# Gated linear attention feeding a mixture of experts: reshapes of the first groups on TensorE instead of through DRAM, and seven weight splits moved into the first expert block

## The chip, the cores and the metric

One core of one Trainium2 chip runs the whole program. The metric is the device time of one execution in microseconds (us); lower is better. Engines: PE (TensorE), DVE (VectorE), ACT (ScalarE), POOL (GpSimd), SP (SyncE, which here only issues DMAs).

## The reference

Two stages. The first is a complex-gated linear attention, step by step over time; the second mixes four two-layer experts.

```python
# q, k, v, a_re, a_im: (4, 8, 768, 48) = batch, heads, time, width
mag = np.sqrt(a_re * a_re + a_im * a_im)
scale = np.minimum(mag, 0.999) / (mag + 1e-06)
a_re_n, a_im_n = (a_re * scale, a_im * scale)
for t in range(S):
    new_re = ar * S_re - ai * S_im
    new_im = ar * S_im + ai * S_re
    S_re, S_im = (new_re + k_t v_t^T, new_im)
    y[:, :, t] = q_t^T S_re
x = y.transpose(0, 2, 1, 3).reshape(3072, 384)
p = domain_probs / domain_probs.sum(-1)
for e in range(4):                     # w1: (4, 384, 1024), w2: (4, 1024, 384)
    out += p[:, e:e+1] * (np.maximum(x @ w1[e], 0) @ w2[e])
```

## The kernel before, in words

The 3072 tokens are cut into NG = 12 groups of 256, each of two chunks of 128 steps. For a group the gates are normalised (`norm`, ACT and DVE), multiplied up along time (`prefix`, DVE), and turned into decayed Q and K (`finish`, DVE and ACT). These come out with (head, width) on the partitions in three slabs of 128. The attention wants each head's 48 rows at partitions 0 to 47 (real part) and 64 to 111 (imaginary part), in `Qst` and `Kst`. `finish` gets them there by writing Q and K to DRAM and reading them back (lines 378 and 383): `k_d<-K`, then `Kst<-k_d`.

`attention` then does for each chunk: `increment` (transposes of K, line 411, a copy to `KT`, line 412, and the state's increment, line 416), `scores` (line 430, masked by DVE, line 433) and `values` (lines 442 and 446, copied to `y`, line 454). y goes to DRAM and comes back as x with 128 rows of (head, width) on the partitions (`y_d<-y`, `xa<-y_d`, lines 486 and 135). `split_x` splits x into a rounded high part `xh` (ACT, line 141) and a rest `xl` (DVE, line 142), since the expert matmuls run in a reduced-precision format (fp32r) three times: high by high, low by high, high by low.

The experts run in two phases. In the first, `moe1` takes a group through the 16 slices of the first two experts, as eight steps of `w1_step` (line 152) and `w2_step` (line 171), one block per group. In the second phase, 512 tokens at a time go through the other two (lines 585 and 598). Weights must be split as x is. `split_w` does this for the first 16: ACT rounds (line 115, `whi`), PE computes the difference with an identity and a negated identity into PSUM (lines 125 and 128, `lp`), and ACT copies it out (line 129, `wlo`). All 16 are split before the first block. The staging tiles for a weight are taken from the tags of `PRE`, two buffers each.

Each engine runs its instructions in order; the order comes from a scheduler that works on the program order and the dependencies. `between(k)` puts a piece of the next group's attention ahead of step k of the current block: for group g the pieces start at step max(2, 5 - g).

Of the kernel before, what the change touches and what calls it, by code (L numbers as in the profile page):

```python
# [11 lines left out]
ALU = mybir.AluOpType  # L12
# [17 lines left out]
NST = 4  # L30
# [25 lines left out]
NPRE = 10  # L56
NMID = 12
# [3 lines left out]
def fast_path(ctx, tc, qkP, aP, vP, probsP, w, out, flag):  # L61
# [8 lines left out]
    ident = const.tile([P, P], F32, name="ident")  # L70
    make_identity(nc, ident)
# [16 lines left out]
    nc.gpsimd.dma_start(pr, probsP.rearrange("(n p) e -> p n e", p=P))  # L88
# [5 lines left out]
    wts = {}  # L94

# [16 lines left out]
    def split_w(i, src, ps=None, prev=None, prev_pe=None):  # L112
        hi = wpool.tile([P, 2 * HD], F32R, tag="whi", name=f"whi{i}")
        lo = wpool.tile([P, 2 * HD], F32R, tag="wlo", name=f"wlo{i}")
        ins = nc.scalar.activation(hi, src, AF.Copy)
        if prev is not None:
            behind(ins, prev)
        if ps is None:
            nc.vector.tensor_tensor(lo, src, hi, op=ALU.subtract)
        else:  # L120
            pool, tag = ps
            for u in range(2):
# [10 lines left out]
    def load_x(g):  # L133
        x = moe.tile([P, NJ, G], F32, tag="x", name=f"xa{g}", bufs=1)
        nc.sync.dma_start(x, y_d[g].rearrange("(j p) t -> p j t", p=P))
        return x

    def split_x(g, x):
        xh = moe.tile([P, NJ, G], F32R, tag="xh", name=f"xha{g}")
        xl = moe.tile([P, NJ, G], F32R, tag="xl", name=f"xla{g}")  # L140
        tc.keep_in_program_order(nc.scalar.activation(xh, x, AF.Copy))  # L141
        tc.keep_in_program_order(nc.vector.tensor_tensor(xl, x, xh, op=ALU.subtract))
# [59 lines left out]
    with ExitStack() as c1:  # L202
# [4 lines left out]
        mask = big.tile([P, C], F32, name="mask")  # L207
# [17 lines left out]
        nc.gpsimd.memset(Qst[32:IM], 0.0)  # L225
        nc.gpsimd.memset(Kst[32:IM], 0.0)
        nc.gpsimd.memset(KT, 0.0)
        nc.gpsimd.memset(P2, 0.0)
        nc.gpsimd.memset(TA, 0.0)

# [22 lines left out]
        def tmp(name):  # L253
            return big.tile([P, 2, NJ * G], F32, tag="tmp", name=name, bufs=TMP)

        def cmul(x, br, bi, shape, nm):
# [6 lines left out]
            v1 = tmp(f"{nm}a")[:, :, :n].rearrange(pat, **kw)  # L263
            v2 = tmp(f"{nm}b")[:, :, :n].rearrange(pat, **kw)
# [11 lines left out]
        def norm(g, A, parts=((0, SEG),), prev=(None, None)):  # L276
            s = tmp(f"s{g}")
            u = tmp(f"u{g}")
            for n, (lo, hi) in enumerate(parts):
# [5 lines left out]
                nc.scalar.activation(L, Af[:, 1], AF.Square)  # L285
# [5 lines left out]
                if n > 0:  # L291
                    behind(ins[0], idn)
                nc.scalar.activation(L, m2, AF.Ln, bias=m2b)
                nc.scalar.activation(y0, L, AF.Exp, scale=-0.5)
# [9 lines left out]
        def prefix(g, A, cuts=(1, NS)):  # L304
            for i in range(1, SEG):
# [6 lines left out]
                nc.vector.tensor_tensor(x[:, 1], z[:, 1, 0], z[:, 0, 1], op=ALU.add)  # L312
            k = 1
            while k < NS:
                nb = MS // (2 * k)
                Al = A[:, :, SEG - 1, :].rearrange("p c (b s) -> p c b s", s=2 * k)
                br, bi = (Al[:, c, :, k - 1:k].broadcast_to([P, nb, k]) for c in range(2))
                cmul(Al[:, :, :, k:], br, bi, [nb, k], f"sk{g}_{k}")
                k *= 2
            As = A.rearrange("p c i (j s) -> p c i j s", j=NJ)  # L320
# [5 lines left out]
        def finish(g, A, qk, parts=((0, CG),)):  # L326
            Q = big.tile([P, 2, NR, C + 1], F32, tag="tmp", name=f"Q{g}", bufs=TMP)
            K = big.tile([P, 2, NR, C], F32, tag="K", name=f"K{g}", bufs=1)
            s = tmp(f"s2{g}")
            u = tmp(f"u2{g}")  # L330
# [19 lines left out]
            for lo, hi in parts:  # L350
# [11 lines left out]
                if hi == CG:  # L362
                    nc.scalar.activation(Q[:, :, :, C].rearrange("p c (j n) -> p c j n", n=CG)[:, :, :, lo:],
                                         A[:, :, SEG - 1, NS - 1::NS].unsqueeze(3).broadcast_to([P, 2, NJ, hi - lo]),
                                         AF.Copy)
                a2, i0, t, kn = (some(x, lo, hi) for x in (a2a, i0a, ta, qk[:, 1]))
# [6 lines left out]
                scr = []  # L373
                for x, nm, w in ((Q, "q", C + 1 if hi == CG else C), (K, "k", C)):
                    dt = dram.tile([2, HD, hi - lo, w], F32, name=f"{nm}_d{g}_{lo}")
                    for c in range(2):
                        xs = x[:, c].rearrange("p (j n) t -> p j n t", n=CG)[:, :, lo:hi, :w]
                        nc.sync.dma_start(dt[c].rearrange("(j p) n t -> p j n t", p=P), xs)
                    scr.append(dt)
                for x, dt in zip((Qst, Kst), scr):  # L380
                    eng = nc.gpsimd if g == 0 and x is Qst else nc.sync
                    for c in range(2):
                        landed = eng.dma_start(x[c * IM:c * IM + D, :, lo:hi, :dt.shape[-1]],
                                                   dt[c].rearrange("(h d) n t -> d h n t", d=D))
            return K, last_act, last_dve, landed
# [10 lines left out]
        def chunk(g, c, K, y):  # L396
# [8 lines left out]
            def increment():  # L405
                if last:
                    return
                for i in range(2):
                    kt_ps = ps_a.tile([P, HD], F32, tag="pa", name=f"ktp{g}_{c}_{i}")
                    for j in range(NJ):  # L410
                        nc.tensor.transpose(kt_ps[:, j * P:(j + 1) * P], K[:, i, j * CG + c, :], ident)  # L411
                    nc.scalar.activation(KT[:, :, i * IM:i * IM + D],
                                         kt_ps.rearrange("p (h d) -> p h d", d=D), AF.Copy)
                d_ps = ps_a.tile([M, H, D], F32, tag="pa", name=f"dp{g}_{c}")
# [409 lines left out]
```

## Time and profile before

| what | value |
|---|---|
| median of 3 runs | 1032.83 us (1031.87 to 1033.28) |
| profiled execution, its own time | 1035.97 us |
| span of its instructions | 1034.2 us |
| PE busy | 988.0 us (96%) |
| DVE busy | 596.5 us (58%) |
| ACT busy | 358.9 us (35%) |
| mean granted PE clock | 0.988 of full speed |

The span is the time from the first to the last instruction on the core. The chain that ended last lies on PE for 88% of it and on DMAs for 6%. "Busy" PE counts a matmul from its issue to its modelled end, at whatever clock it was granted. The rows of a timeline give the start, the time up to the end of the last one merged into the row, the engine, the line, and the idle time before it with what ended it.

### The profile page before, as it was taken

What the parts mean: (1) busy time and instruction counts of PE and PEld (TensorE: products, weight loads), DVE (VectorE), ACT (ScalarE), POOL (GpSimd) and SP (SyncE); (2) the same over time, 40 slices, a digit from 0 to 9 for tenths busy, and PEclk for the clock granted to TensorE, in tenths of its full rate; (3) what the DMA queues carried; (4) which work ended last, traced back from release to release, by engine and by line L of the source; (5) the groups of instructions that cost most, each with busy time, mean ns of one, the idle gap of its engine ahead of it and who ended that gap; (6) DMA issues with size and microseconds to landing.
All of it is one profiled execution on the core that took longest, in us unless ns stands there. A gap on an engine that the chain in (4) does not pass through costs nothing.

```text
span 1034.2 us, 15984 instructions
## 1 busy us (share of the span) xinstructions
PE 988.0 (96%) x6522; PEld 920.8 (89%) x6522; DVE 596.5 (58%) x1201; ACT 358.9 (35%) x647; POOL 27.8 (3%) x51
## 2 busy tenths in 40 slices
PE   4599889999999999999999999999999999999997
PEld 2379889898999999999999999999999999999996
DVE  6788877798988998888982264232232232321221
ACT  6845335352634635355342254121111111111110
POOL 4100000000000000000000000000000000000000
PEclk9989999999999999999999999999999999999999
DMA  7837372745658455483653493012030010100000
GB/s 257 217 113 155 107 197 80 191 115 141 165 139 199 120 149 152 120 203 126 145 123 78 129 360 123 1 41 82 1 110 13 22 71 1 61 1 1 31 1 34
DMA packets 79378, 113.12 MB, mean 109 GB/s; under 512 B 5440, under 2 KB 64496, under 8 KB 79296
## 3 DMA queue, kind: packets, MB, share of 16 engines
q1 hardware_dynamic: 76768, 101.61, 35.5%
q0 software_dynamic: 2528, 10.41, 2.8%
q8 instruction: 53, 0.87, 0.4%
q14 instruction: 29, 0.24, 0.1%
HBM read 74.11 MB, written 37.88 MB: 108 GB/s over the span
## 4 chain that ended last, share of the span: by engine, by line
PE 88%; DMA 6%; DVE 3%; ACT 1%; issue 1%; SPq 0%; DVEq 0%; POOL 0%; ACTq 0%; POOLq 0%
PE pob L598 19%; PE phb L585 19%; PE ph L152 18%; PE po L171 17%; PE sc L430 5%; PE dp L416 2%; PE yp L446 2%; PE yp L442 2%; DMA Kst<-k_d 2%; DMA k_d<-K 1%; PE ktp L411 1%; PE lp L125 1%; DMA pr<-probsP 1%; DMA q_d<-Q 1%; DMA xa<-y_d 1%
## 5 line engine op out<-in xcount | busy, mean ns | idle before, releaser
L591 DVE SCALAR_TENSOR_TENSOR hlb<-phb,hhb 128x512 fp32r<-128x512 f32 x96 | 66.3, 691 | 247.2 <-ACT hhb L590 247.2
L590 ACT ACTIVATE hhb<-phb 128x512 fp32r<-128x512 f32 x96 | 57.4, 598 | 314.2 <-PE phb L585 299.9
L171 PE MATMUL po<-whi,hh 128*128 128x384 f32 x384 | 129.2, 339 | 1.1 <-ACT hh L161 1.1
L598 PE MATMUL pob<-wlo,hhb 128*128 128x384 f32 x384 | 129.3, 337 | 0.0
L171 PE MATMUL po<-wlo,hh 128*128 128x384 f32 x384 | 129.1, 336 | 0.0
L598 PE MATMUL pob<-whi,hhb 128*128 128x384 f32 x384 | 128.9, 336 | 0.0
L171 PE MATMUL po<-whi,hl 128*128 128x384 f32 x384 | 123.1, 338 | 0.5 <-DVE hl L162 0.5
L598 PE MATMUL pob<-whi,hlb 128*128 128x384 f32 x384 | 117.8, 336 | 0.0
L152 PE MATMUL ph<-xha,whi 128*128 128x256 f32 x576 | 105.6, 288 | 4.1 <-ACT xha L141 4.1
L161 ACT ACTIVATE hh<-ph 128x512 fp32r<-128x512 f32 x96 | 57.2, 596 | 149.7 <-PE ph L152 146.1
L152 PE MATMUL ph<-xla,whi 128*128 128x256 f32 x576 | 103.5, 286 | 0.0
L152 PE MATMUL ph<-xha,wlo 128*128 128x256 f32 x576 | 101.4, 284 | 0.0
L162 DVE SCALAR_TENSOR_TENSOR hl<-ph,hh 128x512 fp32r<-128x512 f32 x96 | 66.0, 688 | 51.0 <-ACT hh L161 50.3
L152 PEld LDWEIGHTS ph<-xha,whi 128*128 128x128 f32 x576 | 87.2, 191 | 6.2 <-ACT xha L141 4.9
L585 PE MATMUL phb<-xhb,whi 128*128 128x512 f32 x288 | 91.8, 392 | 0.0
L152 PEld LDWEIGHTS ph<-xla,whi 128*128 128x128 f32 x576 | 83.6, 192 | 0.7 <-issue 0.6
L152 PEld LDWEIGHTS ph<-xha,wlo 128*128 128x128 f32 x576 | 83.2, 191 | 0.2 <-issue 0.2
L585 PE MATMUL phb<-xlb,whi 128*128 128x512 f32 x288 | 83.4, 392 | 0.0
L585 PE MATMUL phb<-xhb,wlo 128*128 128x512 f32 x288 | 82.1, 393 | 0.0
L598 PEld LDWEIGHTS pob<-wlo,hhb 128*128 128x128 f32 x384 | 72.1, 188 | 3.5
L598 PEld LDWEIGHTS pob<-whi,hhb 128*128 128x128 f32 x384 | 72.1, 188 | 3.4
L171 PEld LDWEIGHTS po<-whi,hh 128*128 128x128 f32 x384 | 72.6, 189 | 1.6 <-ACT hh L161 1.4
(142 smaller groups left out, 1568.9 us busy)
## 6 DMA issues: line engine op xcount, KB each, us to landing
wst<-w SPq DMA_DIRECT2D x32, 384.0 KB, 4.8
qk<-qkP SPq DMA_DIRECT2D x24, 384.0 KB, 7.0
acc_d<-acc POOLq DMA_DIRECT2D x24, 384.0 KB, 4.5
prev<-acc_d SPq DMA_DIRECT2D x24, 384.0 KB, 4.8
q_d<-Q SPq DMA_DIRECT2D x22, 387.0 KB, 3.8
Qst<-q_d SPq DMA_DIRECT2D x22, 387.0 KB, 5.6
A<-aP SPq DMA_DIRECT2D x22, 384.0 KB, 8.7
k_d<-K SPq DMA_DIRECT2D x22, 384.0 KB, 3.0
```

Source lines behind the costliest of these rows:

```text
L152: ins = nc.tensor.matmul(ph[:, u, :], wt[:, j * P:(j + 1) * P], xt[:, j, :], start=(n == 0), stop=(n == 3 * NJ - 1))
L161: nc.scalar.activation(hh, ph, AF.Relu)
L162: nc.vector.scalar_tensor_tensor(hl, ph, 0.0, hh, op0=ALU.max, op1=ALU.subtract)
L171: nc.tensor.matmul(po[t], ht[:, u, t * P:(t + 1) * P], wt[:, HD:], start=(i % FE == 0 and n == 0), stop=(i % FE == FE - 1 and n == 2))
L416: ins = nc.tensor.matmul(d_ps[:, h, :], KT[:, h, :], vc[:, h * D:(h + 1) * D], start=True, stop=True)
L430: nc.tensor.matmul(s_ps[:, h, :], Kc[:, hf * 4 + h, :], Qc[:, hf * 4 + h, :], start=True, stop=True)
L442: ins = nc.tensor.matmul(yo, state[g, c][:, h, :], Qc[:, h, :], start=True, stop=False)
L446: ins = nc.tensor.matmul(yo, vc[:, h * D:(h + 1) * D], sc[h // 4][:, h % 4, :], start=first, stop=True)
L585: nc.tensor.matmul(ph, wt[:, j * P:(j + 1) * P], xt[:, j, :], start=(n == 0), stop=(n == 3 * NJ - 1))
L590: nc.scalar.activation(hh, ph, AF.Relu)
L591: nc.vector.scalar_tensor_tensor(hl, ph, 0.0, hh, op0=ALU.max, op1=ALU.subtract)
L598: nc.tensor.matmul(po[t], ht[:, t * P:(t + 1) * P], wt[:, HD:], start=(i % FE == 0 and n == 0), stop=(i % FE == FE - 1 and n == 2))
```

## The change

- **Q and K of the first two groups.** New `pick` multiplies by a 48-column slice of a wide identity (`wide`), 20 matmuls for eight heads, and moves a chunk's rows to their place in PSUM; ACT copies them to `Qst` or `Kst`. Partitions 32 to 63 of PSUM are first set by `blank`, a matmul with a row of zeros, 512 columns wide. For K of a group's first chunk, `turned_back` transposes `KT` back instead. This holds for group 0 (Q of chunk 0, K of both) and group 1 (K of both); Q of chunk 1 of group 0 and all Q of group 1 keep their trip through DRAM (`trip`). `near_attention` orders the pieces. The other groups are as before.
- **x of the first three groups.** New `turn_x` makes x from y by six matmuls with slices of a band matrix per chunk, into PSUM, and `split_x` reads that. `values` has a `blank` per chunk for these groups and copies y once and not in two halves.
- **Weights.** Nine are split ahead of the first block, seven in it, two in front of each of its steps, staged in the two buffers of the tag `acc` alone. The splits ahead of it use two PSUM pools instead of one.
- **Order.** The probabilities' DVE work moves behind the first group's K. `prefix` and `finish` of the first two groups work chunk by chunk. Attention pieces of groups 1 to 4 start at steps 5, 4, 3 and 2. The transposes and the increment of chunk 1 of each group move behind x, for group 0 behind the start of the first block.

```diff
-NPRE = 10
-NMID = 12
+NPRE = 9
+NSEL = 2
+XSEL = 3
+FIRST = {1: 5, 2: 4, 3: 3, 4: 2}
+HOFF = 96
...
+        def blank(ps):
+            n, w = ps.shape[1:]
+            nc.tensor.matmul(ps[32:IM], zero, ident[0:1, 0:1].unsqueeze(2).broadcast_to([1, n, w]),
+                             start=True, stop=True)
+
+        def pick(g, nm, X, dst, s, w):
+            n = 4 if w == C else 3
+            for h0 in range(0, H, n):
+                hs = range(h0, min(h0 + n, H))
+                ps = ps_a.tile([M, len(hs), w], F32, tag="pa", name=f"{nm}p{g}_{s}_{h0}")
+                blank(ps)
+                for h in hs:
+                    js = [j for j in range(NJ) if -D < h * D - j * P < P]
+                    for j in js:
+                        o = 32 + h * D - j * P
+                        for c in range(2):
+                            nc.tensor.matmul(ps[c * IM:c * IM + D, h - h0, :], wide[:, o:o + D],
+                                             X[:, c, j * CG + s, :w], start=(j == js[0]), stop=(j == js[-1]))
+                nc.scalar.activation(dst[:, h0:h0 + len(hs), s, :w], ps, AF.Copy)
...
+            def turned_back():
+                for h0 in range(0, H, 4):
+                    ps = ps_a.tile([M, 4, C], F32, tag="pa", name=f"kp{g}_{c}_{h0}")
+                    for h in range(4):
+                        nc.tensor.transpose(ps[:, h, :], KT[:, h0 + h, :], ident)
+                    nc.scalar.activation(Kst[:, h0:h0 + 4, c, :], ps, AF.Copy)
...
+        def turn_x(g, c, y):
+            xp = ps_a.tile([P, NJ, C], F32, tag="pa", name=f"xp{g}_{c}")
+            for j in range(NJ):
+                ps = [p for p in range(HP) if -HOFF < 2 * D * p - P * j < P]
+                for p in ps:
+                    o = HOFF - (2 * D * p - P * j)
+                    state["xp"] = nc.tensor.matmul(xp[:, j, :], band[:, o:o + P], y[:, p, c * C:(c + 1) * C],
+                                                   start=(p == ps[0]), stop=(p == ps[-1]))
+            return slice(c * C, (c + 1) * C), xp
+
+        def near_attention(g, QK):
...
+            if g == 0:
+                pick(g, "q", Q, Qst, 0, C)
+                yield
+                landed = trip(f"q_d{g}", Q, Qst, 1)()
+            else:
+                landed = trip(f"q_d{g}", Q, Qst)()
+            yield landed
+            turn0()
+            back0()
+            sc0()
+            yield
+            pick(g, "k", K, Kst, 1, C)
+            inc0()
+            val0()
+            sc1()
+            xs = [turn_x(g, 0, y)]
+            val1()
+            xs.append(turn_x(g, 1, y))
+            yield xs
...
                 def between(k, g=g, pieces=pieces, first=first, last=last):
+                    if g == 1:
+                        for i in range(NPRE + 2 * k, min(NPRE + 2 * k + 2, NF1)):
+                            split_w(i, stage1(i, ("acc",)), ((ps_a, "pa"),) * 2, *late)
```

What this does to the order on the engines, at three places. On PE, around the first group's attention, before (`ktp`: transposes of K, `dp`: increment, `lp`: a weight's split, `sc`: scores):

```order
L411 MATMUL ktp_0_0_480<-ident,K_291 128x128 x3
L411 MATMUL ktp_0_1_485<-ident,K_291 128x128 x3
L416 MATMUL dp_0_490<-v_0_476,KT 112x48 x8
L125 MATMUL lp_0_601<-wst_596,ident 128x384
L125 MATMUL lp_1_605<-wst_596,ident 128x384
L430 MATMUL sc_0_0_501<-Qst,Kst 128x128 x4
L430 MATMUL sc_0_1_508<-Qst,Kst 128x128 x4
```

and now (`qp` and `kp_1`: `pick`; line 474: `turned_back`; line 355: `blank`):

```order
L369 MATMUL qp_0_0_304<-Q_235,wide 48x128 x9
L369 MATMUL qp_0_4_317<-Q_235,wide 48x128 x9
L466 MATMUL ktp_0_0_360<-wide,K_236 128x128 x3
L466 MATMUL ktp_0_1_365<-wide,K_236 128x128 x3
L474 MATMUL kp_0_0_370<-wide,KT 112x128 x4
L474 MATMUL kp_0_4_376<-wide,KT 112x128 x4
L494 MATMUL sc_0_0_382<-Qst,Kst 128x128 x4
L494 MATMUL sc_0_1_389<-Qst,Kst 128x128 x4
L355 MATMUL kp_1_0_401<-wide,zero 32x512
L355 MATMUL kp_1_4_414<-wide,zero 32x512
```

The scores now follow transposes of `KT` and not a reading of K from DRAM, and the pieces of `pick` and `blank` stand behind them, ahead of the increment. On ACT, what stands ahead of the copies that these scores wait for (lines 475), now:

```order
L467 ACTIVATE KT<-ktp_0_0_360 128x8x48
L467 ACTIVATE KT<-ktp_0_1_365 128x8x48
L405 ACTIVATE u_234<-s_233,a2b 128x24x16
L406 ACTIVATE u_234<-u_234,a2e 128x24x16
L308 ACTIVATE s_496<-A_204 128x768
L475 ACTIVATE Kst<-kp_0_0_370 112x4x128
L475 ACTIVATE Kst<-kp_0_4_376 112x4x128
```

Two steps of the second chunk's reciprocal (lines 405 and 406) and one square of the next group's gates (line 308) stand between the copies to `KT` and those to `Kst`. On PE behind the first steps of the first block (`ph`: first layer, `po`: second layer), now:

```order
L165 MATMUL ph_1_855<-xla_612,whi_543 128x256 x3
L482 MATMUL dp_1_633<-v_1_302,KT 112x48 x8
L135 MATMUL lp_0_783<-wst_778,wide 128x384
L138 MATMUL lp_0_783<-whi_780,nident 128x384
L135 MATMUL lp_1_787<-wst_778,wide 128x384
L138 MATMUL lp_1_787<-whi_780,nident 128x384
L135 MATMUL lp_0_796<-wst_791,wide 128x384
L138 MATMUL lp_0_796<-whi_793,nident 128x384
L184 MATMUL po_0_0_827<-whi_510,hh_0_823 128x384
```

The second increment of group 0 and the first late split, which stood ahead of the block, now stand between its first and its second layer.

## Rows read from the trace of the kernel before

**Rows 1.** The page, busy time by engine, its row on PE.

```profile
PE 988.0 (96%) x6522; PEld 920.8 (89%) x6522; DVE 596.5 (58%) x1201; ACT 358.9 (35%) x647; POOL 27.8 (3%) x51
```

**Rows 2.** Windows: stretch, length, PE, PEld, DVE, ACT, POOL busy, granted clock, DMA.

```profile
51.50:57.80 6.30, 6.30 (x29) 6.30 (x30) 4.09 (x5) 0.87 (x2) 0.00 (x0) 0.50 0.88 277
...
153.40:156.80 3.40, 3.40 (x18) 2.82 (x17) 2.82 (x8) 0.00 (x0) 0.00 (x0) 0.50 0.52 209
...
245.60:623.90 378.30, 377.55 (x3041) 369.11 (x3041) 290.04 (x600) 165.98 (x305) 9.23 (x17) 1.00 0.56 154
```

**Rows 3.** Timeline from the first group's K to the first block: start, us, engine, line.

```profile
24.17 0.85 ACT L129 ACTIVATE wlo<-lp 128x384 fp32r<-128x384 f32 x2
...
36.14 0.62 ACT L357 ACTIVATE u<-s,a2b 128x384 f32<-128x384 f32 x1
...
36.77 1.03 DVE L371 TENSOR_TENSOR K<-A,u 128x384 f32<-128x384 f32 x2
...
37.31 0.83 ACT L284 ACTIVATE s<-A 128x768 f32<-128x768 f32 x1
...
38.79 0.87 ACT L412 ACTIVATE KT<-ktp 128x384 f32<-128x384 f32 x2
...
39.76 1.74 PE L416 MATMUL dp<-v,KT 128*112 128x48 f32 x16 [1.27 <-issue]
...
51.47 3.76 PE L430 MATMUL sc<-Qst,Kst 112*128 112x128 f32 x16 [8.61 <-DMA Kst<-k_d]
...
74.27 0.62 PE L152 MATMUL ph<-xha,whi 128*128 128x256 f32 x3 [1.45 <-ACT xha L141]
```

**Rows 4.** Timeline: halves of weight splits, and single 384-column passes in fp32r.

```profile
70.17 0.81 PE L125 MATMUL lp<-wst,ident 128*128 128x384 f32 x2
...
70.99 0.83 PE L125 MATMUL lp<-wst,ident 128*128 128x384 f32 x2
...
120.42 0.33 PE L171 MATMUL po<-whi,hh 128*128 128x384 f32 x1
120.59 0.33 PE L171 MATMUL po<-wlo,hh 128*128 128x384 f32 x1
```

**Rows 5.** Timeline: scores at the full clock, and what PE starts behind them.

```profile
103.40 2.02 PE L430 MATMUL sc<-Qst,Kst 112*128 112x128 f32 x16
105.35 0.43 PE L442 MATMUL yp<-Qst,G 112*48 112x128 f32 x4
```

**Rows 6.** Timeline: matmuls 48 columns wide, and a transpose between them.

```profile
62.13 0.39 PE L446 MATMUL yp<-scs,v 128*48 128x128 f32 x4
...
62.35 0.39 PE L442 MATMUL yp<-Qst,G 112*48 112x128 f32 x4
...
62.67 0.33 PE L411 MATMUL ktp<-ident,K 128*128 128x128 f32 x1
...
62.93 0.43 PE L446 MATMUL yp<-scs,v 128*48 128x128 f32 x4
```

**Rows 7.** Timeline: PE's waits behind the start of the first block.

```profile
124.25 0.61 PE L152 MATMUL ph<-xha,whi 128*128 128x256 f32 x3 [2.63 <-ACT xha L141]
...
129.96 0.44 PE L171 MATMUL po<-whi,hh 128*128 128x384 f32 x1 [1.15 <-ACT hh L161]
...
131.43 0.62 PE L171 MATMUL po<-whi,hl 128*128 128x384 f32 x2 [0.51 <-DVE hl L162]
...
151.88 2.36 PE L430 MATMUL sc<-Qst,Kst 112*128 112x128 f32 x16 [2.85 <-DMA Kst<-k_d]
...
196.27 2.43 PE L430 MATMUL sc<-Qst,Kst 112*128 112x128 f32 x16 [2.08 <-DMA Kst<-k_d]
...
242.15 3.65 PE L430 MATMUL sc<-Qst,Kst 112*128 112x128 f32 x16 [1.52 <-issue]
```

**Rows 8.** Timeline of DVE: K of the third group.

```profile
139.94 1.82 DVE L371 TENSOR_TENSOR K<-A,u 128x768 f32<-128x768 f32 x2
```

**Rows 9.** The page, DMA issues: count, size, median us to landing.

```profile
wst<-w SPq DMA_DIRECT2D x32, 384.0 KB, 4.8
```

More of the change, by code (lines that the diff above doesn't have):

```diff
@@ L29 @@
 E1 = 2
-NST = 4
+NST = 6
 TMP = 4
@@ L120, in split_w @@
         else:
-            pool, tag = ps
-            for u in range(2):
+            for u, (pool, tag) in enumerate(ps):
                 us = slice(u * HD, (u + 1) * HD)
@@ L372, in finish, with trip, back @@
                                                        op=ALU.mult)
[L373 to L385, printed above, removed]
+                return last_dve
+            return Q, K, head, tail
+        def trip(nm, X, dst, lo=0, hi=CG):
+            w = X.shape[-1] if hi == CG else C
+            dt = dram.tile([2, HD, hi - lo, w], F32, name=nm)
+            for c in range(2):
+                nc.sync.dma_start(dt[c].rearrange("(j p) n t -> p j n t", p=P),
+                                  X[:, c].rearrange("p (j n) t -> p j n t", n=CG)[:, :, lo:hi, :w])
+            def back():
+                for c in range(2):
+                    landed = nc.sync.dma_start(dst[c * IM:c * IM + D, :, lo:hi, :w],
+                                               dt[c].rearrange("(h d) n t -> d h n t", d=D))
+                return landed
+            return back
         def t_factors():
@@ L403, in chunk, with turned @@
             sc = []
-            def increment():
-                if last:
+            def turned():
+                if last and g >= NSEL:
                     return
@@ L451, in values @@
                     state["pe"] = ins
-                for u in range(2):
-                    us = slice(u * IM, u * IM + D)
+                for us in ((slice(0, M),) if g < XSEL else (slice(0, D), slice(IM, M))):
                     nc.scalar.activation(y[us, :, cs], y_ps[us], AF.Copy)
-            return increment, scores, values
+            return turned, turned_back, increment, scores, values
         def rotate(g):
@@ L486, in attention @@
                 nc.sync.dma_start(yv[u], y[u * IM:u * IM + D])
-            x = load_x(g)
+        def attention(g, QK):
+            y = small.tile([M, HP, G], F32, tag="y", name=f"y{g}")
+            (turn0, _, inc0, sc0, val0), (turn1, _, inc1, sc1, val1) = (chunk(g, c, QK[1], y) for c in range(CG))
+            turn0()
+            inc0()
+            yield sc0()
+            val0()
+            t_factors()
+            xs = [turn_x(g, 0, y)] if g < XSEL else None
+            yield sc1()
+            val1()
+            if g < XSEL:
+                xs.append(turn_x(g, 1, y))
+            store_y(g, y)
+            x = xs or load_x(g)
+            turn1()
             inc1()
@@ L517, in fast_path, with front @@
         qk = load_qk(0)
+        wst.update({i: stage1(i, PRE) for i in range(NST, NST + 2)})
         A.append(load_a(1))
         nrm = norm(0, A[0], parts=halves)
[L520 to L527 removed]
+        cuts = (1, NS // CG, NS)
+        def front(g, A, qk):
+            pre = prefix(g, A, cuts if g < NSEL else (1, NS))
+            Q, K, head, tail = finish(g, A, qk)
+            if g >= NSEL:
+                next(pre, None)
+                la = head(0, CG)
+                ld = tail(0, CG)
+                backs = [trip(f"{nm}_d{g}", X, st) for nm, X, st in (("q", Q, Qst), ("k", K, Kst))]
+                return (Q, K), la, ld, [back() for back in backs][-1], None
+            pieces = near_attention(g, (Q, K))
+            for c in range(CG):
+                next(pre)
+                la = head(c, c + 1)
+                if g == 0 or c == CG - 1:
+                    landed = next(pieces)
+            for c in range(CG):
+                ld = tail(c, c + 1)
+                r = next(pieces) if g == 0 else None
+            return r, la, ld, landed, pieces
+        x, todo = {}, {}
+        x[0], la, ld, landed, todo[0] = front(0, A[0], qk)
+        norm(1, A[1], prev=(la, ld))
+        for i in range(NPRE):
+            split_w(i, wst[i] if i in wst else stage1(i, PRE), ((ps_o, "po"), (ps_h, "ph")))
+        x[0] = split_x(0, x[0])
+        for _ in todo.pop(0):
+            pass
+        late = wts["x"], state["xp"]
+        behind(nc.vector.reduce_sum(prs, pr, axis=mybir.AxisListType.X), ld)
         nc.vector.tensor_scalar(prs, prs, 1e-9, None, op0=ALU.add)
```

152 lines of the change are left out of this document (88 added, 64 removed).

## The prediction

> **What bounds the kernel now.** I read the page first: PE is busy for 988.0 of 1034.2 us [rows 1], so no change to another engine helps unless it removes one of PE's waits, and PE work that is added costs its full time wherever PE never waits. Then the windows: from 245.6 us on PE waits for 0.75 us in 378 [rows 2], and the second phase is denser still. So all that can be won lies ahead of about 246 us. There I read the timeline of PE for two things. One is when the first block starts, which is the first `ph`: 74.27 us [rows 3]. The reader should see the two long trips ahead of it. K is ready at 36.77 + 1.03 = 37.80, and the scores start at 51.47, after 8.61 us in which PE waits for `Kst`; and x comes back from DRAM just ahead of 74.27. The other is what PE waits for behind that start [rows 7]: 2.63, 1.15 and 0.51 us at the second block's start, then 2.85, 2.08 and 1.52 us for the K of groups 2, 3 and 4. Behind each of the last three the granted clock falls to 0.50 for 3.4 us; one such window stands in [rows 2], and there are three. At half the clock 3.4 us of PE work hold 1.7, so 5.1 us are lost beside the waits. From the first block's start the account is simple: every us of PE work moved behind it is paid, every us of wait removed is won.
>
> **Prices on PE.** Half of a weight's split takes 70.99 - 70.17 = 0.82 us [rows 4], a weight 1.64. A half holds two passes of 384 columns in f32 and one in fp32r. The latter is 0.17, the second layer's spacing [rows 4], so an f32 pass is 0.325. A score pass of 128 columns is (105.35 - 103.40) / 16 = 0.122 [rows 5], an f32 matmul has two of them. Four passes of the 48-column matmuls take 62.35 - 62.13 = 0.22 [rows 6], since two heads run side by side. From these: `pick`, 20 matmuls or 40 passes of the same shape, 2.2 us. `blank`, two f32 passes of 512 columns, no row of its own: 512/384 of 0.325 twice, 0.87; the bounds are 0.24 (two passes at a score's price, were its 32 columns to count) and 1.7 (at half the clock). I take 0.87, since columns streamed set the price of the other f32 rows. `turn_x`, 12 passes with full-width weights at 0.122: 1.46 a chunk. `turned_back`, 8 transposes of one pass, at most 0.122 each: 0.98.
>
> **The first block's start.** The DVE chain up to K has the same steps, so I leave K at 37.80, by 2 us either way: ACT does a split in about 1.7 us (0.85 for the two copies of the low part [rows 3], as much for rounding the same 768 columns), and nine of them stand ahead of that chain's end, about as many as before. In the trace of before the copies to `KT` end at 38.79 + 0.87 = 39.66 [rows 3]. Ahead of `Kst` ACT now has two steps like L357 at 0.62 and one square at 0.83 [rows 3], so it is free at 41.73; the transposes of `KT` hide in that. The first `Kst` copy, 512 wide against 0.44 for 384 in the `KT` row, takes 0.58: scores from 42.3, 9.2 us earlier than 51.47.
>
> From there to `ph`: scores of two chunks 2 x 1.95 = 3.9, four `blank` 3.5, `pick` of K 2.2, the increment 1.6 (16 passes in 1.74 less the end of the last [rows 3]), values 0.9 and 1.8, two `turn_x` 2.9, and two copies that PE waits for with their handoffs (y 0.58, xh 0.43) 1.5. Sum 18.3. Then the clock: after the idle stretch of before, 6.3 us ran at 0.50 [rows 2], a loss of 3.15. Now PE has small pieces, `pick` of Q and the transposes, some 4 us, between the last early split and the scores. The loss lies between 0 and 3.15, and I take 1.6, for no row shows such a mixture. The block starts at 42.3 + 18.3 + 1.6 = 62.2: **12.1 us earlier**. Q by `pick` stands ahead of K and is off this path. The DRAM trip of Q's second chunk starts about 1 us behind K; with the 13.7 us that K's took (37.80 to 51.47), among more loads, it would end near 52.5, and the second chunk's scores come 11 us behind the first, near 53: it hides, without much to spare.
>
> **What is paid behind that start.** Seven weights at 1.64: 11.5. The second increment of group 0, once ahead of the block: 1.6. Group 1: `turned_back` 1.0, `pick` 2.2, four `blank` 3.5, `turn_x` 2.9. Group 2: two `blank` 1.7, `turn_x` 2.9. Together 27.3. Changes between column widths come on top: behind a 48-column pair PE starts a transpose 0.10 us late (62.35 + 0.22 to 62.67), and the next pair 0.14 us late (62.67 + 0.12 to 62.93) [rows 6]. The change adds some five such places, 0.6. Sum **27.9**. The Trainium skill (TensorEngine Tiling (Array Packing), Key Properties) says that a change of tiling mode drains TensorE; the trace agrees, with these 0.10 to 0.14 us. If every one of the some 25 borders of a piece drained, that would be 3 and not 0.6.
>
> ACT's copies for the seven weights, 1.7 us each or 12 in all, hide: ACT is busy for 358.9 of 1034.2 us [rows 1]. Were that cover gone, each would hold up a step of the block. The loads hide too, unless the second rival holds.
>
> **What is won behind it.** Block 1 starts later relative to DVE: DVE's chain for group 1 starts a little earlier than before, and block 0 has 23 us more work. In the trace of before K of group 2 was ready at 141.76 [rows 8], 17.5 us behind the second block's start, and its scores had to wait for the trip. Now DVE has the second chunk's `xl`, two steps and K's own 1.82 left at that start, some 5 us. PE has four first layers and three second layers (12 passes of 0.17, 2.1 us; the first about as long) and two increments ahead of those scores, some 18 us. The trip took 10 us (141.76 to 151.88), so it fits. So the waits of 2.85, 2.08 and 1.52 go, the 0.75 behind 245.6, and the three half-clock windows, 5.1: 12.3. The wait at the second block's start doesn't go wholly. There x of group 1 no longer takes a trip, but `turn_x` of its second chunk stands behind the last second-layer matmul, and ACT has two output copies and two steps of group 3 ahead of that copy to `xh`. Between 0 and the 4.3 of before I take 2.4, so 1.9 are won. Sum **14.2**.
>
> **The sum.** -12.1 + 27.9 - 14.2 = **+1.6 us**. The profiled execution's own 1035.97 would become 1037.6; the median, 3.1 lower, 1034.4. That is no change as far as a measurement of this kernel tells one: 0.2%, 2.1 us.
>
> **Rivals.**
>
> *Faster.* The clock never falls in the first attention, since no idle stretch there is as long as the 8.61 us [rows 3] ahead of the half clock; K comes out 2 us earlier because fewer splits stand in ACT's way; and the wait at the second block's start closes. -1.6 - 2 - 2.4 = -6.0 from the forecast, 1028.4. For it: small pieces break the idle stretch. Against it: they fill less than half of it. Chance 0.30.
>
> *Slower: the loads of the late weights.* Weights 9 to 15 are staged in two buffers alone, so 11 to 15 each wait for the split two before them and then for a load. A load took 4.8 us in the middle of 32 [rows 9], and between a split and the next but one PE has about two splits and one step's layer, 5.4 us. If each of five comes 1.5 us late, PE stops 7.5 us in block 0: 1041.9. It decides from a load of about 5.4 us on. Against it: the queues are quiet then. Chance 0.12.
>
> *Slower: the clock stays down.* The first attention runs at half the clock up to its values, about 10 us instead of 3, and a 1.7 us window follows the second block's start: +5, 1039.5. For it: the first window at 0.50 in [rows 2] lasted 6.3 us of steady work. The Trainium skill (TensorE: Matmul & The Clock Gate, Part 4: PE-mode transpose) says that transposes don't count as PE being busy; by that the 14 transposes of this path would not bring the clock up. No row here shows it alone. Chance 0.15.
>
> *The change doesn't do what it says.* DVE still sets when K of groups 2 to 4 is ready, and the 12.3 us are not won: 1046. Chance 0.04.
>
> **Chances.** The forecast has the remaining 0.39, and I count it as within 0.2%. Faster by over that: 0.30. Slower: 0.12 + 0.15 + 0.04 = 0.31. The range, 1027.5 to 1040, takes in the first rival, most of the clock's, and a spread of 2 us in K; the late loads' upper half and the last rival stay outside.
>
> **What would show it.** Right: first scores near 42, first `ph` at 60 to 64 us, no PE wait for `Kst` at groups 2 to 4, no half-clock window there, a second block that starts 130 to 133 us in against 124.25, and a wait ahead of it between 1 and 3 us. Wrong: scores later than 44 (ACT's queue), `lp` in the first block waiting for `wst`, `blank` away from 0.87, or a granted clock of 0.50 between 45 and 60 us for more than 7.

## The result, and the profile after

The changed kernel takes 1037.03 us (median of 19 runs, 1033.42 to 1039.38), the kernel before 1032.74 us beside it (19 runs, 1029.11 to 1035.51). The ratio is 1.0042, 95% interval 1.003 to 1.0054: slower by 0.4%. The forecast was 1034.4, a loss too small to measure; the time lies in the range, on its slow side.

The profiled execution took 1036.68 us, its span 1035.0. The page's row of busy times, against [rows 1]:

```profile
PE 1012.1 (98%) x6754; PEld 936.9 (91%) x6754; DVE 599.1 (58%) x1217; ACT 361.3 (35%) x656; POOL 24.0 (2%) x50
```

PE is busy for 24 us more, and the span grew by 0.8. Where the two meet is in the timeline of PE (start, us, engine, line, with the idle time before in brackets), from the transposes of K to the first block, then at the second block's start and at the scores of group 4:

```profile
35.78 1.22 PE L466 MATMUL ktp<-wide,K 128*128 128x128 f32 x6 [2.72 <-DVE K L422]
37.58 1.96 PE L474 MATMUL kp<-wide,KT 128*112 128x128 f32 x8 [0.58 <-ACT KT L467]
40.17 3.78 PE L494 MATMUL sc<-Qst,Kst 112*128 112x128 f32 x16 [0.63 <-ACT Kst L475]
43.88 3.62 PE L355 MATMUL kp<-wide,zero 1*32 1x512 f32 x4
47.43 3.69 PE L369 MATMUL kp<-K,wide 128*48 128x128 f32 x40
51.05 1.77 PE L482 MATMUL dp<-v,KT 128*112 128x48 f32 x16
52.75 1.04 PE L355 MATMUL yp<-wide,zero 1*32 1x512 f32 x2
...
61.69 1.60 PE L543 MATMUL xp<-y,band 112*128 112x128 f32 x12 [0.69 <-ACT y L519]
...
63.88 0.62 PE L165 MATMUL ph<-xha,whi 128*128 128x256 f32 x3
...
134.17 0.61 PE L165 MATMUL ph<-xha,whi 128*128 128x256 f32 x3 [0.38 <-ACT xha L152]
...
240.71 2.02 PE L494 MATMUL sc<-Qst,Kst 112*128 112x128 f32 x16 [1.21 <-issue]
```

Against [rows 3]: the scores start at 40.17 instead of 51.47, the first block at 63.88 instead of 74.27. Against [rows 7]: the second block starts at 134.17 instead of 124.25, with 0.38 us of wait instead of 2.63; of the waits for K of groups 2, 3 and 4 only the last is left, 1.21. The windows (length, busy PE, PEld, DVE, ACT, POOL, granted clock, DMA share, GB/s) tell of the clock, against [rows 2]:

```profile
40.20:50.10 9.90, 9.90 (x46) 6.61 (x48) 9.43 (x16) 3.12 (x4) 0.00 (x0) 0.50 0.65 199
50.10:63.80 13.70, 13.01 (x132) 10.44 (x128) 6.95 (x19) 4.75 (x10) 0.00 (x0) 1.00 0.14 35
107.50:114.90 7.40, 7.40 (x69) 4.40 (x69) 4.96 (x20) 1.19 (x2) 0.00 (x0) 1.00 0.01 2
115.00:118.40 3.40, 3.40 (x32) 3.04 (x29) 1.54 (x9) 0.33 (x1) 0.00 (x0) 0.51 0.00 0
135.00:250.00 115.00, 113.73 (x920) 108.65 (x919) 98.07 (x210) 47.08 (x87) 2.17 (x4) 1.00 0.58 153
```

From its first scores on, the first attention runs at half the clock for 9.9 us, with PE busy all the while; a half-clock stretch of 3.4 us at 115 us is new; the three behind the waits for K are gone. Cut at the two block starts, the profiled executions compare as follows (the forecast's terms sorted into the same cuts: of the 27.9 paid, 4.6 belong to group 2 and so to the last row; the 1.9 won at the second block's start stand in the middle one):

| stretch | before | after | change | forecast |
|---|---|---|---|---|
| up to the first block | 74.27 | 63.88 | -10.4 | -12.1 |
| first to second block | 49.98 | 70.29 | +20.3 | +21.4 |
| second block to the end | 909.9 | 900.8 | -9.1 | -7.7 |
| span | 1034.2 | 1035.0 | +0.8 | +1.6 |

So against this profile of the kernel before, the three terms hold to 2 us each. The question for the runs was why the medians differ by 4.3 us where the profiles differ by 0.8, and what each part costs. The ratios below are always to the kernel before, run on the same chip; the changed kernel's own 1.0042 is the number to hold them against. The ratio of the run with selection for one group leaves out one of its six executions, which took 4346 us at a granted clock of 0.221.

### The profile page after: what moved, and what is told of

The parts are those of the page before. It is cut to its first block, busy times and chain, and to the rows that moved or that the text cites. A ratio compares the mean times of both kernels' runs of the same rounds, so it can differ in the third digit from the quotient of the medians.

```text
span 1035.0 us, 16428 instructions
## 1 busy us (share of the span) xinstructions
PE 1012.1 (98%) x6754; PEld 936.9 (91%) x6754; DVE 599.1 (58%) x1217; ACT 361.3 (35%) x656; POOL 24.0 (2%) x50
## 4 chain that ended last, share of the span: by engine, by line
PE 94%; ACT 2%; DVE 2%; DMA 1%; issue 0%; SPq 0%; ACTq 0%
PE pob L737 19%; PE phb L724 19%; PE ph L165 19%; PE po L184 19%; PE sc L494 5%; PE dp L482 3%; PE yp L512 2%; PE yp L508 2%; PE lp L135 2%; PE ktp L466 1%; PE xp L543 1%; DMA wst<-w 1%; PE kp L369 1%; PE yp L355 1%; PE kp L355 1%; DMA q_d<-Q 1%
## 5 line engine op out<-in xcount | busy, mean ns | idle before, releaser
L165 PE MATMUL ph<-xla,whi 128*128 128x256 f32 x576 | 100.8, 283 | 0.0
L184 PEld LDWEIGHTS po<-wlo,hh 128*128 128x128 f32 x384 | 72.5, 189 | 0.5 <-issue 0.2
```

Of the source, the lines that this page charges most:

```text
L165: ins = nc.tensor.matmul(ph[:, u, :], wt[:, j * P:(j + 1) * P], xt[:, j, :], start=(n == 0), stop=(n == 3 * NJ - 1))
L184: nc.tensor.matmul(po[t], ht[:, u, t * P:(t + 1) * P], wt[:, HD:], start=(i % FE == 0 and n == 0), stop=(i % FE == FE - 1 and n == 2))
```

## Experiments

**The kernel before, again.** No edit.

> The kernel before, unchanged, beside itself. The question: its median moved 4.3 us below the changed kernel's, its one profiled execution only 0.8 us (span 1034.2 against 1035.0). Theory: the profiled execution of before was a slow draw, about 3 us over its median, because the executions differ in how long TensorE stays at half its clock; then the spans listed run by run should spread from about 1028 to 1034 us and the granted clock should rise as the span falls. Rival: profiling itself adds these 3 us to this kernel; then the spans of all the timed runs should lie near 1031 with little spread, and a second profile should again show 1034.

Measured: median 1032.57, ratio 0.9992 (0.9976 to 1.0007). The 12 spans reach from 1026.6 us (mean clock 0.990) to 1034.0 (0.985); over all 92 timed runs of this kernel here, span and clock have a correlation of -0.65. The second profile has a span of 1031.3: scores at 50.38, first block at 72.62, second at 122.32. The theory holds in its main part: the first profile was a slow draw, not an effect of profiling. Its reason, the clock, does not explain these two profiles: the slower has the higher clock (0.988 against 0.985), and its first scores, behind the trip of K, come 1.1 us later. By the same three cuts the change is -8.7, +20.6 and -8.2 against this second profile, together +3.7, which is close to the 4.3 of the medians.

**Halves instead of blanks.** Ten of the twelve blanks go, those of K and y; the two of Q stay. (The text before the run says eight of ten; its sum, four and six, counts the ten.) The rows between the halves are zeroed by POOL.

```diff
...
-                blank(ps)
+                if len(parts) == 1:
+                    blank(ps)
...
-                nc.scalar.activation(dst[:, h0:h0 + len(hs), s, :w], ps, AF.Copy)
+                for us in parts:
+                    nc.scalar.activation(dst[us, h0:h0 + len(hs), s, :w], ps[us], AF.Copy)
...
-                if g < XSEL:
-                    blank(y_ps)
...
+        nc.gpsimd.memset(Kst[32:IM], 0.0)
...
+                nc.gpsimd.memset(y[32:IM], 0.0)
```

> The changed kernel without eight of its ten blanks: K of chunk 1 and y are copied out of PSUM in two halves, and the rows between them are zeroed once in SBUF by POOL. Theory: a blank costs PE 0.97 us at the full clock and 1.8 at half, and nothing hides it. Ahead of the first block four of them go, two at half the clock (3.6 + 1.9 us), less about 1 us for a second y copy that PE waits for twice: first block near 59.5 us instead of 63.88. Behind it six go, 5.8 us. Sum about -10 us, 1027. Rival: ACT's four more copies are on the path ahead of the block and the group's border, PE waits instead; then the first block starts at 62 or later and the sum is -6 or less, 1031.

Measured: median 1027.66, ratio 0.9943 (0.9925 to 0.9962): 9.4 us under the changed kernel, as the theory has it, and 0.6% under the kernel before. But not by its own steps: K ended at 40.05, 3.9 later, and the first block started at 61.99, no more than 1.9 earlier. PE's timeline of this run shows one reason, ahead of K:

```profile
9.03 2.90 PE L135 MATMUL lp<-wst,wide 128*128 128x384 f32 x4 [9.03 <-DMA wst<-w]
11.86 3.62 PE L356 MATMUL qp<-wide,zero 1*32 1x512 f32 x4
15.41 2.93 PE L135 MATMUL lp<-wst,wide 128*128 128x384 f32 x4
```

POOL's added zeroing made the row of zeros late, so the two blanks of Q now stand among the early splits (3.62 us at the low clock) and not ahead of them. The greater gain lies behind the block's start: 64.9 us from first to second block instead of 70.29. A blank there costs 0.97 at the full clock, four of them 3.9; and no half-clock stretch came at 115 us (1.7).

**Early blanks back in front.**

```diff
         nc.gpsimd.memset(Qst[32:IM, :, 1:], 0.0)
-        nc.gpsimd.memset(Kst[32:IM], 0.0)
...
                                     compare_op=ALU.not_equal, fill=1.0, base=base, channel_multiplier=1)
+        nc.gpsimd.memset(Kst[32:IM], 0.0)
```

> As the run with copies in halves, but POOL zeroes the rows of Kst behind the band, so that the two blanks of Q, which wait for POOL's row of zeros, stand ahead of the first split again, as in the changed kernel. There the granted clock rose at 12.55 us and K of the first group ended at 36.19; without them in front it rose at 21.27 and K ended at 40.05. Theory: the early blanks bring the clock up some 8 us sooner, the splits and with them ACT's copies run ahead, and K is 3.9 us earlier: first block near 58 us, 1027.7 - 3.9 = 1023.8. Rival: the clock's rise is by chance or K's delay has another cause: K at 40, 1027.7.

Measured: median 1025.56, ratio 0.9923 (0.9897 to 0.9949). K ended at 36.16 and the first block started at 59.01, 3.0 us earlier than in the run before it, but only about 2 of them are left in the median, with ratios whose intervals overlap, and 1.1 in the span: K of group 4 came too late for the earlier PE, a wait of 1.57 us at 230.86 and a half-clock stretch behind it. Whether the clock's earlier rise (12.41 against 21.27 us) or the place of the blanks among the splits made K early, these two runs don't tell apart.

**Two early blanks in the kernel before.**

```diff
+        zero = big.tile([1, IM - 32], F32, name="zero")
+        nc.vector.memset(zero, 0.0)
+        for n in range(2):
+            early = ps_a.tile([M, 4, C], F32, tag="pa", name=f"early{n}")
+            nc.tensor.matmul(early[32:IM], zero, ident[0:1, 0:1].unsqueeze(2).broadcast_to([1, 4, C]),
+                             start=True, stop=True)
```

> The kernel before with two blanks alone (a row of zeros times a row of ones into 512 columns that nobody reads), which stand first on TensorE and run while it would wait for the first weight. Theory: the clock is then up near 12.5 us instead of 20.3 to 21.5 as in the two profiles of before, the early splits and ACT's copies run ahead, K of the first group comes 1 to 2 us earlier than 37.8 to 38.1, and the kernel gains about 2 us (ratio 0.998): a part of the changed kernel's earlier first block has nothing to do with its selection matmuls. Rival: K of before hangs on DVE's chain and the trip alone: no earlier first block, ratio 1.000.

Measured: median 1033.28, ratio 1.001 (0.999 to 1.003); K at 37.70, clock up at 20.23. The theory fell, the rival holds. PE was busy from 5.47 to 11.95 us here, then waited 2.48 for ACT's rounding of the first weight. In the changed kernel, whose early splits have two PSUM pools, PE goes from 5.91 to 14.52 without a gap. So the blanks alone bring nothing; that the second pool is what matters beside them was not tried.

**The idle stretch ahead of K filled.**

```diff
...
-                pick(g, "q", Q, Qst, 0, C)
+                ins = pick(g, "q", Q, Qst, 0, C)
+                idle = ps_a.tile([P, 2, 192], F32, tag="pa", name="idle")
+                for n in range(13):
+                    mm = nc.tensor.matmul(idle[:, 0, :], ident, wide, start=True, stop=True)
+                    behind(mm, ins)
```

> The changed kernel with 13 matmuls more, 192 columns wide, whose result nobody reads, between pick of Q and the transposes of K, where PE waits from 33.06 to 35.78 us. Theory: the clock falls at 36.4 us because PE stood idle ahead of it; with the stretch filled it stays up until the scores end at least, and from the scores to the first block it takes about 19 us instead of 23.7: -4 to -5 us, 1032.5. Rival: the pieces behind the scores (blank with one row, pick with 48 columns) bring or keep the clock down by themselves: it falls all the same, later, and the gain is under 1.5 us, 1036.

Measured: median 1038.95, ratio 1.0083 (1.0052 to 1.0115): no gain, rather a loss. And yet the clock was up where the theory has it, as PE's timeline shows:

```profile
34.36 4.49 PE L556 MATMUL idle<-wide 128*128 128x192 f32 x26
38.69 0.82 PE L467 MATMUL ktp<-wide,K 128*128 128x128 f32 x6
40.15 1.09 PE L475 MATMUL kp<-wide,KT 128*112 128x128 f32 x8 [0.65 <-ACT KT L468]
41.49 2.05 PE L495 MATMUL sc<-Qst,Kst 112*128 112x128 f32 x16 [0.25 <-ACT Kst L476]
43.47 1.04 PE L355 MATMUL kp<-wide,zero 1*32 1x512 f32 x2
44.44 1.30 PE L369 MATMUL kp<-K,wide 128*48 128x128 f32 x20
...
60.70 0.62 PE L165 MATMUL ph<-xha,whi 128*128 128x256 f32 x3
...
238.27 3.01 PE L495 MATMUL sc<-Qst,Kst 112*128 112x128 f32 x16 [1.91 <-issue]
```

The added matmuls overran K by 2.8 us, but then scores, blanks and `pick` ran at the full clock: 19.2 us from the scores to the first block instead of 23.7, a start 3.2 us earlier. That the idle stretch held the clock down before is likely from this, but not shown. Two later profiles speak against it as the whole cause. These are windows of this run, of the filled kernel with later pieces (below; the same up to the first block), and of the kernel with halves, early blanks and later pieces (below), with PE's timeline of the last:

```profile
30.90:34.30 3.40, 3.40 (x32) 3.04 (x26) 3.40 (x10) 0.82 (x2) 0.00 (x0) 0.50 0.02 5
34.40:60.70 26.30, 24.71 (x215) 19.58 (x214) 20.02 (x43) 13.50 (x24) 0.00 (x0) 1.00 0.36 109
...
41.30:46.40 5.10, 5.10 (x40) 3.15 (x40) 4.73 (x11) 3.72 (x5) 0.00 (x0) 1.00 1.01 302
46.50:49.80 3.30, 3.30 (x27) 2.91 (x26) 3.23 (x3) 0.94 (x2) 0.00 (x0) 0.50 0.16 60
...
36.20:39.50 3.30, 2.72 (x13) 2.27 (x13) 1.95 (x6) 3.02 (x6) 0.00 (x0) 0.50 0.40 120
40.50:47.40 6.90, 6.90 (x88) 6.47 (x88) 6.69 (x14) 4.74 (x8) 0.00 (x0) 1.00 0.88 275
...
35.99 1.47 PE L469 MATMUL ktp<-wide,K 128*128 128x128 f32 x6 [2.77 <-DVE K L425]
38.04 1.79 PE L477 MATMUL kp<-wide,KT 128*112 128x128 f32 x8 [0.58 <-ACT KT L470]
40.49 2.02 PE L497 MATMUL sc<-Qst,Kst 112*128 112x128 f32 x16 [0.67 <-ACT Kst L478]
```

In the first, the clock was at half earlier, behind the wait for Q (2.47 us). In the second, it fell at 46.46 among blanks and `pick`, though the stretch was filled and PE had been busy since 41.28. In the third, PE stood idle ahead of K as in the changed kernel, and yet the clock was back before the scores. The three profiles with the idle stretch and with blanks behind the scores (the changed kernel and the runs with `NSEL = 1` and `XSEL = 2`) have 13.7 to 17.1 us at half the clock; the third one here has 3.4, the run with halves and early blanks 10.2, though the two run the same program up to the first block. So the length differs between executions, and that the blanks and `pick` keep the clock down, as the rival has it, is not ruled out.

The second block started 5.2 us earlier (128.95). By 276 us all of it but 0.8 was gone: 1.91 us of wait at K of group 4, its half-clock stretch (1.7), 0.58 behind the second block's start, and smaller ones.

**Three weights more ahead of the first block.** `-NPRE = 9`, `+NPRE = 12`.

> The changed kernel with 12 weights split ahead of the first block instead of 9, four in it instead of seven. Theory: the three take 4.9 us of PE out of the block, and ahead of it PE stands idle for 5 us that they fill; but ACT's copies for them (5.1 us) stand ahead of its steps for K, which comes out about 2 us later: net -3, 1034. Rival: ACT's copies are paid wholly on the way to K (K near 41, scores near 45): 1037, no change. Other rival: PE's filled stretches also keep the clock up: -6, 1031.

Measured: median 1039.21, ratio 1.0076 (1.0048 to 1.0104): not faster but slower. K ended at 38.74, 2.5 us later, as expected, and the first block started at 64.94. The second started at 125.75, 8.4 us earlier than in the changed kernel. Then, in this order at groups 2, 3, 4 and 5:

```profile
149.16 2.02 PE L494 MATMUL sc<-Qst,Kst 112*128 112x128 f32 x16 [0.77 <-issue]
...
195.50 3.15 PE L494 MATMUL sc<-Qst,Kst 112*128 112x128 f32 x16 [1.17 <-issue]
...
242.96 2.85 PE L494 MATMUL sc<-Qst,Kst 112*128 112x128 f32 x16 [1.63 <-issue]
...
290.78 1.60 PE L494 MATMUL sc<-Qst,Kst 112*128 112x128 f32 x10 [2.62 <-issue]
```

Waits of 6.2 us in all, and three half-clock stretches at 196, 244 and 292 (5.1 us lost): the pattern of [rows 7] is back. K of group 2 ended at 139.87, in the changed kernel at 139.10: a PE that is 8.4 us ahead at the second block's start doesn't make it earlier. This is the mechanism of the forecast, run backwards.

**What DVE waits for.** Why, then, did PE's gain last where the blanks went? K of group 2 ended at 132.33 and 129.38 there. Its row in the changed kernel, with 12 weights ahead, and with copies in halves and early blanks:

```profile
137.29 1.82 DVE L422 TENSOR_TENSOR K<-A,u 128x768 f32<-128x768 f32 x2
...
138.04 1.82 DVE L422 TENSOR_TENSOR K<-A,u 128x768 f32<-128x768 f32 x2
...
127.57 1.82 DVE L425 TENSOR_TENSOR K<-A,u 128x768 f32<-128x768 f32 x2
```

Counted from the start of the first block it ends 75.2 us later in the changed kernel, 74.9 with 12 weights ahead, 73.3 in the filled run, 70.3 and 70.4 in the two runs with halves. So K follows the start of the first block and not the PE work in it: an earlier start moves K along, splits taken out of the block don't. In the run with halves and early blanks, the earlier start is 4.9 of the 9.7 us that K came earlier. For the rest, the waits of DVE on the way to K (engine, line, releaser; us in total, times, longest) are, in the changed kernel from 100 to 139 us:

```profile
DVE scs L497 <- PE sc L494: 2.8, 2, 2.7
DVE G L487 <- PE dp L482: 2.2, 1, 2.2
```

with 12 weights ahead, from 100 to 140:

```profile
DVE scs L497 <- PE sc L494: 1.8, 2, 1.4
DVE G L487 <- PE dp L482: 1.7, 1, 1.7
```

and with copies in halves and early blanks, from 96 to 130, where the list has neither of the two:

```profile
DVE s L311 <- ACT s L310: 1.2, 1, 1.2
DVE u L421 <- ACT u L409: 1.0, 1, 1.0
DVE hl L175 <- ACT hh L174: 1.0, 1, 1.0
DVE s L406 <- ACT s L403: 0.9, 1, 0.9
```

Group 1's mask (`scs`) and state (`G`) stand in DVE's queue among group 2's steps. The second scores and the increment they wait for stand behind the blanks and `pick` on PE. So a blank there costs 0.97 on PE and, by these waits, holds up DVE too, and with it K of the next group. The two waits are 5.0 us in the changed kernel, as much as that rest; but no run takes out the blanks alone, since the halves change ACT's copies as well.

**Selection for one group.** `-NSEL = 2`, `+NSEL = 1`.

> The changed kernel, but Q and K of the second group take the trip through DRAM as all later groups do (selection for one group instead of two). Theory: K of the second group is ready by 93.3 us, its trip takes about 10 us, and its scores stand near 104 us, so the trip hides; what goes is turned_back (1.0), pick (2.5) and two blanks (1.9): -5.4 us, 1031.6. Rival: the trip comes back late, PE waits 2 to 3 us for Kst and falls to half its clock behind the wait (another 1.7): 1036, no gain.

Measured: ratio 1.012 (1.0082 to 1.0157), the worst of all. Both theories missed the time. The rival's wait for K of group 1 came (2.63, with a half-clock stretch behind it), but the greater waits are behind the second block's start:

```profile
106.88 3.58 PE L494 MATMUL sc<-Qst,Kst 112*128 112x128 f32 x16 [2.63 <-DMA Kst<-k_d]
135.17 1.77 PE L482 MATMUL dp<-v,KT 128*112 128x48 f32 x16 [2.77 <-ACT KT L467]
144.06 1.74 PE L466 MATMUL ktp<-wide,K 128*128 128x128 f32 x6 [4.96 <-DVE K L422]
```

K of group 1 ended at 95.43, 2.1 us later than in the changed kernel, and its trip landed at 106.7, not 104. DVE's queue passes that on: from 95 to 145 us it waits for PE's scores of group 1

```profile
DVE scs L497 <- PE sc L494: 4.9, 3, 3.8
```

and for ACT, with steps of group 2 behind these waits. K of group 2 ended at 144.78 instead of 139.10. (DVE's waits on the way make 11.6 us, 9.9 in the changed kernel; with the 2.1 of K of group 1 that is 3.8 of the 5.7, and the rest stays open.) Its transposes stand early in the second block, PE's queue waits behind them, and the clock is at half for 13.65 us. So in this kernel selection for the second group is worth far more than the trip that it saves: without it, DVE's next K slips.

**x of the third group through DRAM.** `-XSEL = 3`, `+XSEL = 2`.

> The changed kernel, but x of the third group goes through DRAM (band matmuls for two groups instead of three). What goes on PE: two band steps of 1.46 and two blanks of 0.97, 4.9 us. Theory: y of that group ends near 173 us, and with some 8 us of trip and split x is there near 181, while the block before ends near 179: a wait of 2 to 3 us takes half of it back: about -2.5, 1034.5. Rival: the trip hides wholly, -4.9, 1032. Other rival: the wait also brings a half-clock window (1.7): -1, 1036.

Measured: median 1034.58, ratio 1.0005 (0.9991 to 1.0018), 2.4 us under the changed kernel. The time is the theory's, its reason only in part: x was there after 0.50 us of wait, and the second block took 44.2 us instead of 49.3, all of the 4.9. The third then took 46.9 instead of 44.7, with a wait of 0.75 for K of group 3. Again PE ran into the next K.

**Attention pieces one step later**, in the filled kernel, in the one with halves and early blanks, and in the latter with x of the third group through DRAM (`XSEL = 2`).

```diff
-FIRST = {1: 5, 2: 4, 3: 3, 4: 2}
+FIRST = {1: 5, 2: 4, 3: 4, 4: 3, 5: 3}
```

> The run with the filled stretch, and the attention pieces of groups 3, 4 and 5 one step later in their blocks (steps 4, 3, 3 instead of 3, 2, 2). In that run the first block started 3.2 us earlier and the half-clock window at 115 us was gone, and yet its profile ended as late as the changed kernel's; between 129 and 276 us the 5 us were lost again. Theory: K of groups 2 to 5 is set by DVE's chain and its trip, not by PE; a PE that runs ahead waits there (1.91 us at group 4) and pays a half-clock window (1.7). A step later (4 us) K is there first: no such wait, 1034, 5 under that run. Rival: DVE's chain is slower than PE on the whole, so the waits only move on to the next groups: 1038 to 1039, as that run.

> The run with copies in halves and early blanks, and the attention pieces of groups 3, 4 and 5 one step later. Theory: its wait of 1.57 us for K of group 4 and the half-clock window behind it (1.7) go: 1025.6 - 3.3 = 1022.3. Rival: the waits move on to later groups: 1025 or more.

> As the run before it, and x of the third group through DRAM. Theory: two band steps of 1.46 and one more pair of copies go, 2.9 us of PE (the blanks are gone already), and the trip hides but for half a microsecond: 1022.3 - 2.5 = 1019.8. Rival: PE only runs into the K of the next groups: 1022.

Measured: filled 1036.50, ratio 1.0044 (1.002 to 1.0067), 2.5 us under the filled run, with intervals that overlap, between theory and rival; halves 1027.28, ratio 0.9936 (0.9919 to 0.9953), no gain; with x of the third group 1023.09, ratio 0.9901 (0.9879 to 0.9924), nearer the rival's 1022 than the theory's 1019.8, with a wait of 1.83 us for K of group 6. In the first two the waits for K were gone from the profile, as the theory has it, but at the start of the fourth block x was late. The filled one:

```profile
227.56 0.62 PE L165 MATMUL ph<-xha,whi 128*128 128x256 f32 x3 [1.68 <-ACT xha L152]
```

and the one with halves:

```profile
218.28 0.62 PE L165 MATMUL ph<-xha,whi 128*128 128x256 f32 x3 [2.48 <-ACT xha L152]
```

Neither theory nor rival had this. The x that is late is that of group 3, whose pieces moved from step 3 to 4; at step 3 it had hidden both its trips, to 0.24 us, in the run with early blanks, where the greater wait was for K of group 4. Moving groups 4 and 5 alone was not tried.

**The same with group 6 a step later too.** `FIRST` gains `6: 3`.

> As the run with x of the third group through DRAM, with the pieces of group 6 one step later too, since its profile waits 1.83 us for K of group 6. Theory: that wait goes: 1023.1 - 1.8 = 1021.3. Rival: it moves to another border, 1023.

Measured: median 1023.87, ratio 0.9924 (0.9907 to 0.9941): the wait moved to group 7 (1.08 at 362.04). The rival holds; the intervals of the two overlap. The run with x of the third group through DRAM and later pieces has the lowest median of all, 1% under the kernel before, but it is not told apart from this one, nor from the run with early blanks.

## Why the prediction was right, and where not

- **K and the first scores.** I left K at 37.80; it ended at 36.19, and the scores started at 40.17, not 42.3. Within the 2 us allowed; the steps from K to the scores took 4.0 instead of 4.5.
- **The clock in the first attention** was the term that was mis-sized: 1.6 us taken, 5.0 measured (9.9 us of PE work at half the clock). This was the rival "the clock stays down", in its size and its place but for the start, which was earlier. For that reason the sign that I had named, half the clock for more than 7 us between 45 and 60, did not show: it was 5.1 us there. With the idle stretch ahead of K filled, the path from scores to block is 19.2 us, against 18.3 without a loss in the forecast; but the other profiles above keep the idle stretch from being shown as the whole cause, which stays open. The Trainium skill (TensorE: Matmul & The Clock Gate, Part 4: PE-mode transpose) says that transposes don't count as PE being busy in the same way. The traces don't bear this out as the reason: in the filled run the same 14 transposes passed at the full clock, and in the one with halves and later pieces PE ran nothing else from 35.99 to 39.83 us, and the clock, at half since 36.11, rose at 39.53.
- **Prices**, at the full clock by the starts in the filled run's timeline: `blank` 44.44 - 43.47 = 0.97 (taken 0.87), `pick` twice 45.67 - 44.44, 2.46 (2.2), `turn_x` 1.43 (1.46). The sums hold.
- **The second block's start**: 134.17, a little over the 130 to 133 forecast, since the first block started later. Its wait was 0.38 and not 2.4; the 2 us won so were spent on the half-clock stretch at 115, which I had not forecast in this place.
- **The waits for K** at groups 2 and 3 and the three half-clock stretches behind them went as forecast; 1.21 at group 4 stayed. That DVE and the trip set K, and that PE work in the block ahead of it is therefore free up to the wait, is shown by the run with 12 weights ahead.
- **Late loads of weights**: PE waits for none in the first block. That rival was wrong.
- **What failed** is the last step: "the median, 3.1 lower". I took over from one profile to the other that it lies 3.1 us over its median. The first profile of before was a slow draw; the changed kernel's lies at its own median (1036.68 against 1037.03). Against the second profile of before the same three cuts give +3.7, and the first of them misses the forecast by 3.4 us, as much as the clock's term. So the likeliest case, no change, was off by the spread of one profiled execution, which I had not put into the sum.
- **Luck.** That the span came within 0.8 us of the forecast is in part luck. The clock cost 3.4 us more than taken, but K and ACT's steps behind it came 2.1 earlier; the stretch at 115 cost 1.7, but the wait at the second block's start was 2.0 shorter. The sum had none of the four at its size.

## What to carry to other kernels

Work that is moved in front of a wait for another engine's chain is free up to that wait, and work taken away there is won only up to it: look for the next thing that is late before pricing either. A helper matmul is priced by its columns and by who stands behind it: here a matmul with weights of one row by 32 columns and 512 columns streamed cost 0.97 us on PE and, as it seems, held DVE's queue as well, where the second copy of y on ACT that replaced it made PE wait 0.6 us more ahead of the first block (1.30 against 0.69) and 0.2 at the second. A sum of 1 or 2 us on one profile needs a second profile of the same kernel before its sign means anything.

## What had not been expected of the hardware

The granted clock fell at 115 us in the changed kernel though PE had been busy without a gap for 50 us; ahead of it stood 7.4 us of blanks, `pick` and an increment (107.5 to 114.9, above). In the other profiles with the same pieces there and no wait ahead of them it did not fall, and none of the profiles of the five kernels without these blanks has a half-clock stretch at that place. But the filled kernel with later pieces has one at 46.46, with 3.2 us of blanks and `pick` ahead of it. What decides it stays open.

In some kernels the executions differ almost wholly by the clock. The 12 runs of the filled kernel reach from 1034.21 us (mean clock 0.998) to 1049.65 (0.985), and time and clock there have a correlation of -1.0; in the kernel before it is -0.65. No profile was taken of such a long execution, so which waits make it is not known.
